# A ring of three fixed score tiles, a new pipeline order, and SyncE places of their own for X copies and the experts' first fetches

## The chip, the cores and the metric

The kernel runs on one core of a Trainium2 chip. The metric is the device time of one execution in microseconds (us). Of the kernel before there are three timed runs and one profiled execution; of the profiled one there is a trace of every engine and DMA queue. The engines are called PE (TensorE), PEld (its weight loads), DVE (VectorE), ACT (ScalarE), POOL (GpSimd) and SP (SyncE, which issues most DMAs).

## What is computed

Attention over 8 batches of 8 heads, 576 tokens and 64 dimensions a head, with rotary embedding of q and k; its output is the input of a mixture of 8 experts of which each token takes one.

```
q_rot, k_rot = rotate(q), rotate(k)
scores = q_rot @ k_rot.T / sqrt(64)
attn = exp(scores - max); attn /= attn.sum + 1e-9
x = (attn @ v)  as 4608 rows of 512
logits = x @ w_gate + modality_bias[modality_id]
e_idx, gate_w = argmax(logits), softmax(logits)[e_idx]
out[mask_e] = gate_w * (relu(x[mask_e] @ w1[e]) @ w2[e])   for each expert e
```

Everything is float32. w1[e] is 512x1024, w2[e] is 1024x512.

## The kernel before, in words

**Work and tiles.** The attention goes over 32 pairs of heads, n = 0 to 31, four pairs to a batch. For one pair SP loads q and k, already laid out with their half-rotated copies, into one of two buffers `R` (`LD`, L121, trace name `ST`), and v (`LV`, L129 and L130). From the third pair on POOL applies the rotary embedding in three passes of 128x1216 (`T1` L212, `T2` L214, `R` L216). The result is split for float32r products: ACT writes the high part (`HI`), POOL the low part (`LO`, L220), both into `HL`. SP copies each part with its two head halves swapped into `SW` (`SWH`, `SWL`, L228, two DMAs each). A buffer `R` is loaded anew for pair n once `LO` of pair n-2 has read it, so `LD` waits on SP for that.

**Scores.** A pair has nine score tiles u = 0 to 8 (`S0` to `S8`, L242), each of two PSUM banks and three products (high-high, low-high, high-low); tile 8 holds the tails of both heads. Behind each come the row minimum on DVE (`MN`, L250; q carries the factor -1/8, so it is the maximum of the scores) and the exponential on ACT (`EX`, L257), which reads the minimum as its bias. Then PE transposes the exponentials by 128x64 blocks into further PSUM tiles of the same ring (`F0` to `F3`, `FA`, `FB`, L263). Bank 0 of such a tile is copied out by ACT (`A_F..`), bank 1 by DVE (`B_F..`, L294), into `PH` and `PD`. The product with v goes in two halves (`AVA`, `AVB`, L318), is copied to `oT` by ACT (`OTA`, `OTB`), turned back and multiplied with the gate's weights by PE (`OUTA`, `OUTB`, L349 and L352), and scaled by DVE into the batch's tile of X (`EVA`, `EVB`, L363 to L369) with the reciprocals of the sums (`RE` on ACT L333, `RI` on DVE). `RE` runs once a pair, which makes it a mark of the period.

The tiles of scores and of transposes come from one pool of three (`psS`, L108): the pool hands them out in turn, and the first write into a tile waits for everything that used it before.

**A batch's end.** After the fourth pair of a batch, X goes to memory with five DMAs on SP (`xout`, one at L374, four at L378). The routing of the batch is a chain of 13 small steps, `rk` 0 to 12, from one engine to the next (L389 to L443): POOL at step 2 (L402 to L405) and step 5 (L416 to L418), ACT at step 3 (`ex`, L409) and step 6 (`ee`, L422), DVE between, PE at step 8, and `oi` on POOL at the end. Five scatters on POOL (L451) then write token and gate into the expert's table `TAB`.

**The experts.** Tokens go through the experts in blocks of 256. The first eight blocks are full blocks of the first six batches; they are planned while the last pairs run (28 small steps `plan`, after pair 23). For a block, SP reads the plan's registers (`m_plan`), fetches the block's rows of the table (`ix`, L583, and `xi`, four DMAs at L586), and, when the expert changes, its w1 and w2 (`m_load1`, `m_load2`). POOL computes indices (`iy`, L592) and gathers the rows of X (L594), eight indirect DMAs per block; DVE transposes them (L635), ACT and DVE split them, and PE computes w1 (L653) and w2 (L670). The first block's fetches, splits and w1 products are placed among the last pairs of the attention.

**The order.** Every job of a pair has a key; job J of pair n is at `key + PER*n`, all jobs are sorted by that, and the order of each engine's queue follows it word by word. On PE, ACT, DVE and POOL this holds for the whole kernel, on SP up to the end of the last pair's own jobs (`dmas.close()`). The routing's keys start at `r0`, a little behind `max(EVA, EVB)` of the batch's fourth pair. `xout` has the key `r0 - 0.01` (L748). Jobs of the experts are placed by `Z(key, ...)`, relative to pair 31. In that block all seven later plans and three table fetches have one key, `ix_` (L775 to L778). The dependencies themselves are found and turned into semaphore waits automatically, whatever the order. The keys are times of a model only in so far as they give the order: an engine does what is next in its queue as soon as its waits are met.

With PER = 14.117 and its keys, the order on SP within a period is `LD`, `SWL`, `LV`, `xout` (each fourth), `SWH`; on POOL `T2`, `R`, `T1`, `LO`; on PE, starting at `S0`: `S0 S5 AVA FA F0 F1 S7 S6 S8 OUTB OUTA F2 F3 FB S4 S2 S1 AVB S3`, where the last five belong to the next pair's scores and this pair's product.

Of the kernel before, what the change touches and what calls it, by code (L numbers as in the profile page):

```python
# [8 lines left out]
F32 = mybir.dt.float32  # L9
# [4 lines left out]
ALU = mybir.AluOpType  # L14
# [4 lines left out]
P = 128  # L19
# [10 lines left out]
K0, Q0, T0, K1 = 0, 288, 800, 928  # L30


PER = 14.117
KEYS = {
# [5 lines left out]
    "FB": 8.50, "A_FB": 9.18, "B_FB": 9.40, "AVA": 14.99, "OTA": 19.19, "AVB": 10.83, "OTB": 16.59, "OUTA": 21.06,  # L40
    "EVA": 24.37, "OUTB": 20.30, "EVB": 21.39, "RE": 11.08, "RI": 16.32, "T1": -34.98, "T2": -27.91, "R": -24.56,
    "LO": -16.92, "HI": -18.39, "SWH": -16.92, "SWL": -12.25, "LD": -41.49, "LV": -10.91,
}
AT = dict(
    rk=(0, 0.6, 1.5, 4.7, 5.5, 6.3, 6.9, 7.5, 9.6, 10.4, 11.2, 14.4, 15.2),
    pl=1.5,
    sc=(10.5, 9.0),
    ix=8.0,
    rows=3.0,
    rows1=-9.0,  # L50
    gap=(3.0, 1.3),
    tr=3.5,
    te=-8.0,
    hi=(-14.0, -9.0, -5.0, -1.0),
# [9 lines left out]
def tile_attention_moe(ctx: ExitStack, tc: tile.TileContext, qk, v, mod, wg, mb, w1, w2, rope, cf, ci, out):  # L64
# [40 lines left out]
    W1 = [wp.tile([P, 4, F], F32R, name=f"W1{c}") for c in "HL"]  # L105
    att = ExitStack()
    pp = att.enter_context(tc.tile_pool(name="pp", bufs=1))
    psS = att.enter_context(tc.tile_pool(name="psS", bufs=3, space=PSUM))  # L108
    psA = att.enter_context(tc.tile_pool(name="psA", bufs=2, space=PSUM))

    st = {}
# [4 lines left out]
    Vs = [pp.tile([P, 2, 5, 64], F32, name=f"V{i}") for i in range(2)]  # L116

    RW = pp.tile([P, 4, 2, 72], F32, name="RW")

    def load(n):  # L120
        nc.sync.dma_start(out=Rs[n % 2], in_=qk[n])  # L121
# [109 lines left out]

    def scores(n, u):
        d = st[n]
        ps = psS.tile([P, 2, 512], F32, name="ps", tag="ps")
        heads = (0, 1) if u == 8 else (u % 2,)
        q0 = T0 if u == 8 else Q0 + u // 2 * P
        L = [(hh, wq, wk) for hh in heads for wq, wk in ((0, 0), (1, 0), (0, 1))]
        for m, (hh, wq, wk) in enumerate(L):
            for g in range(2):
                t = d["HL" if g == hh else "SW"][g * 64:g * 64 + 64]  # L240
                k0 = K1 if g else K0
                nc.tensor.matmul(ps[:, g, 0:288], t[:, wq, q0:q0 + P], t[:, wk, k0:k0 + 288], start=(m == 0), stop=(m == len(L) - 1))  # L242
        if "sum" not in d:
            d["sum"] = sm.tile([P, 9], F32, name="sum", tag="sum")
        d["S", u] = ps

    def rowmin(n, u):
        d = st[n]
        mn = sm.tile([P, 1], F32, name="mn", tag="mn", bufs=6)
        nc.vector.tensor_reduce(mn, d["S", u][:, :, 0:288], op=ALU.min, axis=AX.XY)  # L250
        d["m", u] = mn

    def expo(n, u):
# [6 lines left out]

    def tpose(ps, g, c, src, k0):
        r = slice(g * 64, g * 64 + 64)
        nc.tensor.transpose(ps[:, g, c:c + 64], src[r, k0:k0 + P], idf[r, r])  # L263

    def fill(n, f):
        d = st[n]
        ps = d[f] = psS.tile([P, 2, 512], F32, name="ps", tag="ps")
        if f[1] in "0123":
            j = int(f[1])
            for i in range(8):  # L270
                for g in range(2):
                    tpose(ps, g, i * 64, PJ[j], (S + 64) * (i // 4) + i % 4 * P)
        elif f == "FA":
            for j in range(2):
                for g in range(2):
                    tpose(ps, g, j * 64, PJ[j], 512)
        else:
            for kt in range(4):
                for g in range(2):
                    tpose(ps, g, kt * 64, P4, 64 + g * 64 + kt * P)  # L280
            for g in range(2):
                tpose(ps, g, 256, P4, (1 - g) * S)
            for j in (2, 3):
                for g in range(2):
                    tpose(ps, g, 192 + j * 64, PJ[j], 512)
# [275 lines left out]
    def bank(kind):  # L561
        if kind in banks:
            return banks[kind].tile([P, 512], F32, name=f"ps{kind}", tag=f"ps{kind}")
        if not spare:
            ps = psS.tile([P, 2, 512], F32, name="ps", tag="ps")
            spare.extend(ps[:, i, :] for i in (1, 0))
        return spare.pop()

# [11 lines left out]
    def m_ix(s):  # L580
        d = ms[s]
        ix = d["ix"] = ixp.tile([P, 2, 2], I32, name="ix", tag="ix")
        nc.sync.dma_start(out=ix, in_=TAB[bass.ds(d["r"], BLK), :].rearrange("(p t) w -> p t w", t=2))  # L583
        xi = d["xi"] = ixp.tile([P, 8, 2], I32, name="xi", tag="xi")
        for i in range(4):
            nc.sync.dma_start(out=xi[i * 32:i * 32 + 32], in_=TAB[bass.ds(d["r"], BLK), :].rearrange("(q g) w -> q g w", g=8))  # L586
# [93 lines left out]
    def J(k_, nm, n, f, *a):  # L680
        jobs.append((k_ + PER * n, len(jobs), f, a))
# [32 lines left out]
    for n in range(NPAIR):  # L714
        def K_(nm, f, *a):
            J(K[nm], nm, n, f, *a)

        for u in range(9):
            K_(f"S{u}", scores, n, u)
            K_(f"MN{u}", rowmin, n, u)  # L720
            K_(f"EX{u}", expo, n, u)
        for f in ("F0", "F1", "F2", "F3", "FA", "FB"):
            K_(f, fill, n, f)
            for g in range(2):
                K_(f"{'AB'[g]}_{f}", evac, n, f, g)
        for w in range(2):
            c = "AB"[w]
            K_(f"AV{c}", AV, n, w)
            K_(f"OT{c}", avout, n, w)
            K_(f"OUT{c}", outp, n, w)  # L730
            K_(f"EV{c}", ev, n, w)
        for w in range(2):
            K_("R" + "EI"[w], rsum, n, w)
        if n > 1:
            for part, nm in enumerate(("T1", "T2", "R", "HI", "LO")):
                K_(nm, rope_, n, part)
            for i in range(2):
                K_("SW" + "HL"[i], swap, n, i)
            K_("LV", loadv, n)
        if n > 3:  # L740
            K_("LD", load, n)
        if n % 4 == 1:
            J(r0 - PER, "bias", n, bias, n // 4)
        if n % 4 == 3:
            g = route(n // 4)
            early = n == NPAIR - 9
            r1 = r0 + AT["rk"][-1] + 0.02
            J(r0 - 0.01, "xout", n, xout, n // 4)  # L748
            steps = [(next, g, None)] * NRK
# [12 lines left out]
            for j, (f, *a) in enumerate(scats):
                J(r1 + AT["sc"][early] * j, "sc", n, f, *a)


    def Z(k_, f, *a):
        J(k_, "moe", z, f, *a)

    A = AT
    w1_ = max(r1 + AT["pl"] * 28 - 8 * PER, K["T1"] + 0.1, K["LO"] + 0.1 - PER)  # L770
    ix_ = max(w1_, r1 + A["sc"][1] * 4 + A["ix"] - 8 * PER)
    rows_ = ix_ + A["rows"]
    ga_ = {s * 8 + i: rows_ + A["gap"][0] * i if s == 0 else A["rows1"] + A["gap"][1] * (s * 8 - 8 + i) for s in range(3) for i in range(8)}
    tr_ = [ga_[4 * t + 3] + A["tr"] for t in range(2)]
    te_ = [max(t + 0.6, A["te"]) for t in tr_]  # L775
    Z(w1_, each, m_plan, (0,))
    Z(w1_, each, m_load1, *((0, g) for g in range(4)))
    Z(ix_, m_ix, 0)  # L778
    Z(ix_, each, m_plan, *((s,) for s in range(1, NA)))
    Z(ix_, each, m_ix, *((s,) for s in range(1, 4)))  # L780
    for i in range(8):
        for s in range(3):
            Z(max(ga_[8 * s + i], te_[1] + 0.01) if s == 2 else ga_[8 * s + i], m_gather, s, i // 4, i % 4)
    Z(max(K["LO"] + 0.1, w1_ + 10), each, m_load2, *((0, g) for g in range(4)))
    for g in range(4):
        Z(max(A["hi"][g], w1_ + 10), m_hi, 0, g)
        Z(max(A["hi"][g], w1_ + 10) + 1.3, m_lo, 0, g)
# [1 line left out]
        Z(tr_[t], m_tr, 0, t)  # L789
        Z(te_[t], m_tre, 0, t)  # L790
    for g in range(4):
        l1 = max(A["l1"][g], A["hi"][g] + 1.5, w1_ + 11.5, te_[1] + 1.5)
        Z(l1, m_l1, 0, g)
        Z(l1 + A["l1e"], m_l1e, 0, g)
        Z(end + A["sp2"][g], m_split, 1, g)
# [180 lines left out]
```

## Time and profile before

| | |
|---|---|
| median of 3 runs | 1020.57 us |
| lowest, highest | 1018.56, 1023.85 us |
| profiled execution | 1011.64 us, its span 1009.9 us |
| granted TensorE clock, mean | 0.963 |
| busy: PE, PEld | 924.1 us (92%), 749.4 us (74%) |
| busy: DVE, ACT, POOL | 679.9, 634.1, 666.8 us |

The span runs from the first to the last instruction on the chip. A busy PE includes matmuls at half clock, so its 92% is not all useful work; a stage has to be read with its granted clock beside it. The attention takes the first 564 us or so, with the experts' first blocks from about 482 us on; the rest is the experts.

### The profile page before, as it was taken

How to read it: one execution, taken by the hardware profiler on the slowest of the kernel's cores; microseconds unless marked ns; L12 is line 12 of the kernel's file. 1: busy time of each engine (PE TensorE's matmuls, PEld its weight loads, DVE VectorE, ACT ScalarE, POOL GpSimd, SP SyncE). 2: the span in 40 equal slices, each digit the busy share in tenths (PEclk: the TensorE clock that was granted, in tenths of full speed). 3: DMA queues.
4: the chain of work that ended last, by engine and by line, in shares of the span. 5: the costliest groups of instructions: out<-in, count | busy, mean ns of one | idle time of the engine just before them, and what ended most of it. 6: DMA issues, size and time to landing. Idle time of an engine off the chain costs nothing. (4 is left out here: it accounts for less than half of the span.)

```text
span 1009.9 us, 24801 instructions
## 1 busy us (share of the span) xinstructions
PE 924.1 (92%) x9248; PEld 749.4 (74%) x9248; DVE 679.9 (67%) x1158; ACT 634.1 (63%) x1299; POOL 666.8 (66%) x498
## 2 busy tenths in 40 slices
PE   1999999999999999989558999999999999999996
PEld 1767677676776767757335779888899998888995
DVE  6678678576776777767438277866667766666671
ACT  2778678686877778767437265556566555565661
POOL 7776777887787878889467036666566666655500
PEclk9999899898999999999868899999999999999998
DMA  9666757567575766856554043112261431611100
GB/s 280 188 174 169 194 129 222 133 174 208 139 214 142 191 197 163 216 135 174 161 138 89 2 147 131 43 54 60 66 199 34 135 115 49 215 53 42 45 23 15
DMA packets 73102, 132.70 MB, mean 131 GB/s; under 512 B 29535, under 2 KB 49407, under 8 KB 67984
## 3 DMA queue, kind: packets, MB, share of 16 engines
q1 hardware_dynamic: 62576, 110.33, 39.4%
q0 software_dynamic: 9536, 19.48, 6.5%
q8 instruction: 75, 1.23, 0.6%
q10 hardware_dynamic: 864, 1.25, 0.4%
q14 instruction: 51, 0.42, 0.2%
HBM read 140.59 MB, written 19.77 MB: 159 GB/s over the span
## 5 line engine op out<-in xcount | busy, mean ns | idle before, releaser
L257 ACT ACTIVATE P<-ps,mn 128x576 f32<-128x576 f32 x288 | 210.9, 739 | 126.6 <-DVE mn L250 126.6
L250 DVE TENSOR_REDUCE mn<-ps 128x1 f32<-128x576 f32 x288 | 203.3, 750 | 90.5 <-PE ps L242 90.4
L242 PE MATMUL ps<-SW 64*128 64x288 f32 x960 | 183.3, 326 | 38.3 <-DMA SW<-HL 27.2
L594 POOL DMA_INDIRECT XG<-X,iy x152 | 179.7, 1182 | 49.8 <-issue 39.8
L653 PE MATMUL psH<-HL,W1H 128*128 128x256 f32 x1152 | 202.6, 279 | 0.0
L242 PE MATMUL ps<-HL 64*128 64x288 f32 x960 | 186.7, 323 | 15.4 <-ACT HL L203 15.2
L242 PEld LDWEIGHTS ps<-SW 64*128 64x128 f32 x960 | 139.9, 196 | 61.5 <-DMA SW<-HL 29.8
L653 PEld LDWEIGHTS psH<-HL,W1H 128*128 128x128 f32 x1152 | 176.7, 188 | 1.6
L242 PEld LDWEIGHTS ps<-HL 64*128 64x128 f32 x960 | 143.3, 196 | 27.9 <-ACT HL L203 15.2
L653 PE MATMUL psH<-HL,W1L 128*128 128x256 f32 x576 | 160.8, 279 | 0.7 <-DVE W1L L200 0.7
L318 PE MATMUL pa<-PH,V 128*64 128x256 f32 (+1 forms) x1024 | 150.3, 439 | 0.0
L200 DVE TENSOR_TENSOR W1L<-ST,W1H 128x1024 fp32r<-128x1024 f32 x76 | 90.1, 1222 | 83.3 <-ACT W1H L203 83.3
L674 POOL DMA_INDIRECT out_dram<-y,ix x38 | 40.8, 1074 | 155.1 <-ACT y L673 132.0
L670 PE MATMUL psY<-W2H,SW 128*128 128x512 f32 x304 | 120.3, 396 | 1.3 <-ACT W2H L203 1.3
L670 PE MATMUL psY<-W2L,SW 128*128 128x512 f32 x304 | 120.3, 396 | 0.5 <-DVE W2L L200 0.5
L318 PEld LDWEIGHTS pa<-PH,V 128*64 128x64 f32 x1024 | 71.9, 145 | 55.6 <-issue 22.2
L294 DVE COPY PH<-ps 128x512 f32<-128x512 f32 (+1 forms) x160 | 94.0, 632 | 26.2 <-PE ps L263 25.6
L263 PEld LDWEIGHTS ps<-idf,P 64*128 64x128 f32 x2624 | 89.9, 142 | 26.7 <-ACT P L257 14.5
L653 PEld LDWEIGHTS psH<-HL,W1L 128*128 128x128 f32 x576 | 108.3, 188 | 0.9 <-DVE W1L L200 0.9
L220 POOL TENSOR_TENSOR HL<-ST,HL 128x1216 fp32r<-128x1216 f32 x30 | 83.0, 2768 | 37.7 <-ACT HL L203 34.5
L263 PE MATMUL ps<-idf,P 64*128 64x64 f32 x2624 | 99.6, 229 | 7.1 <-ACT P L257 6.7
L203 ACT ACTIVATE PH<-ps 128x512 f32<-128x512 f32 (+1 forms) x160 | 79.8, 555 | 33.3 <-PE ps L263 32.1
(159 smaller groups left out, 1619.4 us busy)
## 6 DMA issues: line engine op xcount, KB each, us to landing
ST<-in_moe_w_dram SPq DMA_DIRECT2D x152, 512.0 KB
ST<-in_qk_dram SPq DMA_DIRECT2D x31, 1216.0 KB
SW<-HL SPq DMA_DIRECT2D x124, 232.0 KB
V<-in_v_dram SPq DMA_DIRECT2D x64, 128.0 KB
X<-X SPq DMA_DIRECT2D x8, 1024.0 KB
XG<-X,iy POOLq DMA_INDIRECT x152, 2.9
xi<-TAB SPq DMA_DIRECT2D x76, 2.0 KB
V<-in_v_dram SPq DMA_DIRECT2D x64, 16.0 KB
```

The costliest lines, as they stand in the source:

```text
L200: nc.vector.tensor_tensor(o, a, b, op=ALU.subtract)
L203: return nc.scalar.activation(o, i, AF.Copy, scale=scale)
L220: e.tensor_tensor(d["HL"][:, 1, c], a, d["HL"][:, 0, c].bitcast(F32), op=ALU.subtract)
L242: nc.tensor.matmul(ps[:, g, 0:288], t[:, wq, q0:q0 + P], t[:, wk, k0:k0 + 288], start=(m == 0), stop=(m == len(L) - 1))
L250: nc.vector.tensor_reduce(mn, d["S", u][:, :, 0:288], op=ALU.min, axis=AX.XY)
L257: nc.scalar.activation(p.rearrange("p (a b) -> p a b", a=2), ps[:, :, 0:288], AF.Exp, bias=d.pop(("m", u)), scale=-1.0, accum_out=d["sum"] ...
L263: nc.tensor.transpose(ps[:, g, c:c + 64], src[r, k0:k0 + P], idf[r, r])
L294: mine.append((nc.vector.tensor_copy if g else acopy)(o, i).ins)
L318: nc.tensor.matmul(pa[hh * 64:hh * 64 + 64, 0:c1 - c0], d["V"][:, hh, kt, :], r, start=(kt == 0), stop=(kt == 4))
L594: nc.gpsimd.indirect_dma_start(out=XG[s % 2][:, t, g, :], out_offset=None, in_=X.rearrange("n (i f) -> (n i) f", f=P)[0:rows], in_offset=b ...
L653: nc.tensor.matmul(ps[:, i, :], w[:, c, f0:f0 + P], x[:, c, :], start=(m == 0), stop=(m == 11))
L670: nc.tensor.matmul(ps, hx[:, c, t * P:(t + 1) * P], w[:, c, :], start=(m == 0), stop=(m == 23))
```

## The change

- The three score tiles are fixed now, one PSUM pool with `bufs=1` and three names. `ring()` hands them out in turn. A tile's last row minimum is remembered, and PE's writes into the tile are declared free of it: they wait for the exponential, which itself waited for the minimum. Waits of a refill are by the regions written, no longer by the whole pool tile.
- PER and all keys of the pair's jobs are new. The order on PE within a period is now `S0 AVB S2 S5 S4 OUTB OUTA F3 F0 FA F2 FB F1 S8 S1 S6 AVA S7 S3` (from `S8` on the next pair's scores and this pair's `AVA`; `AVB` is the previous pair's); on POOL `T2`, `R`, `T1`, `LO`; on SP `SWL`, `LD`, `LV`, `SWH`, `XO` (each fourth).
- `xout` has a key of its own, `XO`.
- `xi` is fetched with one DMA whose source is repeated four times, in place of four DMAs.
- Plans, table fetches and loads of the experts' first blocks have a key each. The first block's w1 products come behind the last scores and transposes.

```diff
-PER = 14.117
+PER = 14.438
 KEYS = {
...
+    "S0": 0.00, "MN0": 1.75, "EX0": 3.14, "S1": -4.26, "MN1": -2.77, "EX1": -1.95, "S2": 3.22, "MN2": 3.92, "EX2":
+    4.72, "S3": -0.39, "MN3": 0.21, "EX3": 2.42, "S4": 4.17, "MN4": 5.26, "EX4": 6.18, "S5": 3.77, "MN5": 4.59,
+    "EX5": 5.46, "S6": -3.75, "MN6": -2.10, "EX6": -1.23, "S7": -0.95, "MN7": 0.88, "EX7": 1.70, "S8": -5.22, "MN8":
+    -4.02, "EX8": -2.91, "F0": 6.57, "A_F0": 7.38, "B_F0": 7.37, "F1": 8.69, "A_F1": 9.59, "B_F1": 9.85, "F2": 7.62,
+    "A_F2": 8.41, "B_F2": 8.41, "F3": 5.81, "A_F3": 6.90, "B_F3": 6.78, "FA": 7.17, "A_FA": 7.86, "B_FA": 7.96,
+    "FB": 8.21, "A_FB": 8.89, "B_FB": 9.00, "AVA": 11.22, "OTA": 13.98, "AVB": 14.84, "OTB": 18.19, "OUTA": 19.77,
+    "EVA": 25.51, "OUTB": 19.01, "EVB": 20.38, "RE": 11.27, "RI": 15.89, "XO": 27.00, "T1": -32.78, "T2": -26.38,
+    "R": -23.03, "LO": -15.27, "HI": -18.83, "SWH": -17.41, "SWL": -11.79, "LD": -39.33, "LV": -10.14,
 }
 AT = dict(
...
-    ix=8.0,
-    rows=3.0,
-    rows1=-9.0,
-    gap=(3.0, 1.3),
...
+    w1=(1.0, 5.7, 8.0, 10.2),
+    w2=(-8.0, -5.0, -2.0, 1.0),
+    plan=(-99.0, -15.0, 4.0, 6.0, 8.0, 10.0, 12.0, 14.0),
+    ix=(-16.5, -9.5, 4.0, 6.0),
+    rows=4.0,
+    gap=1.3,
 )
...
-    psS = att.enter_context(tc.tile_pool(name="psS", bufs=3, space=PSUM))
+    psS = att.enter_context(tc.tile_pool(name="psS", bufs=1, space=PSUM))
...
+    RING = [psS.tile([P, 2, 512], F32, name=f"ps{i}") for i in range(3)]
+    lastmin = [None] * 3
+    turn = [0]
+
+    def ring():
+        i = turn[0] % 3
+        turn[0] += 1
+        seen, lastmin[i] = lastmin[i], None
+        return i, RING[i], seen
+
+    def free(inst, seen):
+
+        if seen is not None:
+            tc.declare_no_dep(inst.ins, seen, reason="the exponential waited for the minimum")
...
-                nc.tensor.matmul(ps[:, g, 0:288], t[:, wq, q0:q0 + P], t[:, wk, k0:k0 + 288], start=(m == 0), stop=(m == len(L) - 1))
+                free(nc.tensor.matmul(ps[:, g, 0:288], t[:, wq, q0:q0 + P], t[:, wk, k0:k0 + 288],
+                                      start=(m == 0), stop=(m == len(L) - 1)), seen)
...
-        nc.tensor.transpose(ps[:, g, c:c + 64], src[r, k0:k0 + P], idf[r, r])
+        free(nc.tensor.transpose(ps[0][:, g, c:c + 64], src[r, k0:k0 + P], idf[r, r]), ps[1])
...
-        for i in range(4):
-            nc.sync.dma_start(out=xi[i * 32:i * 32 + 32], in_=TAB[bass.ds(d["r"], BLK), :].rearrange("(q g) w -> q g w", g=8))
+        nc.sync.dma_start(out=xi, in_=TAB[bass.ds(d["r"], BLK), :].rearrange("(q g) w -> q (g w)", g=8).unsqueeze(0).to_broadcast([4, 32, 16]))
...
-            J(r0 - 0.01, "xout", n, xout, n // 4)
+            K_("XO", xout, n // 4)
...
-    ix_ = max(w1_, r1 + A["sc"][1] * 4 + A["ix"] - 8 * PER)
...
+    ix_ = [max(w1_, r1 + A["sc"][1] * 4 + 8 - 8 * PER, t) for t in A["ix"]]
+    ga_ = {s * 8 + i: ix_[s] + A["rows"] + A["gap"] * i for s in range(3) for i in range(8)}
...
-    Z(w1_, each, m_load1, *((0, g) for g in range(4)))
-    Z(ix_, m_ix, 0)
-    Z(ix_, each, m_plan, *((s,) for s in range(1, NA)))
-    Z(ix_, each, m_ix, *((s,) for s in range(1, 4)))
+    for g in range(4):
+        Z(w1_ + A["w1"][g], m_load1, 0, g)
+        Z(max(K["LO"] + 0.1, w1_ + 10, A["w2"][g]), m_load2, 0, g)
+    for s in range(NA):
+        if s:
+            Z(max(ix_[0], A["plan"][s]), m_plan, s)
+        if s < 4:
+            Z(max(ix_[s], A["plan"][s] + 0.01), m_ix, s)
...
-    Z(max(K["LO"] + 0.1, w1_ + 10), each, m_load2, *((0, g) for g in range(4)))
...
-        l1 = max(A["l1"][g], A["hi"][g] + 1.5, w1_ + 11.5, te_[1] + 1.5)
+        l1 = max(A["l1"][g], A["hi"][g] + 1.5, w1_ + 11.5, te_[1] + 1.5, max(K[f] for f in K if f[0] in "SF") + 0.1 * g + 0.1)
```

More of the change, by code (lines that the diff above doesn't have):

```diff
@@ L30 @@
 K0, Q0, T0, K1 = 0, 288, 800, 928
-PER = 14.117
+PER = 14.438
 KEYS = {
[5 rows of a table removed]
-    "FB": 8.50, "A_FB": 9.18, "B_FB": 9.40, "AVA": 14.99, "OTA": 19.19, "AVB": 10.83, "OTB": 16.59, "OUTA": 21.06,
-    "EVA": 24.37, "OUTB": 20.30, "EVB": 21.39, "RE": 11.08, "RI": 16.32, "T1": -34.98, "T2": -27.91, "R": -24.56,
-    "LO": -16.92, "HI": -18.39, "SWH": -16.92, "SWL": -12.25, "LD": -41.49, "LV": -10.91,
[5 rows of a table added]
+    "FB": 8.21, "A_FB": 8.89, "B_FB": 9.00, "AVA": 11.22, "OTA": 13.98, "AVB": 14.84, "OTB": 18.19, "OUTA": 19.77,
+    "EVA": 25.51, "OUTB": 19.01, "EVB": 20.38, "RE": 11.27, "RI": 15.89, "XO": 27.00, "T1": -32.78, "T2": -26.38,
+    "R": -23.03, "LO": -15.27, "HI": -18.83, "SWH": -17.41, "SWL": -11.79, "LD": -39.33, "LV": -10.14,
 }
@@ L233, in scores @@
         d = st[n]
-        ps = psS.tile([P, 2, 512], F32, name="ps", tag="ps")
+        ri, ps, seen = ring()
+        d["ring", u] = ri
         heads = (0, 1) if u == 8 else (u % 2,)
@@ L249, in rowmin @@
         mn = sm.tile([P, 1], F32, name="mn", tag="mn", bufs=6)
-        nc.vector.tensor_reduce(mn, d["S", u][:, :, 0:288], op=ALU.min, axis=AX.XY)
+        lastmin[d["ring", u]] = nc.vector.tensor_reduce(mn, d["S", u][:, :, 0:288], op=ALU.min, axis=AX.XY).ins
         d["m", u] = mn
@@ L262, in tpose @@
         r = slice(g * 64, g * 64 + 64)
-        nc.tensor.transpose(ps[:, g, c:c + 64], src[r, k0:k0 + P], idf[r, r])
+        free(nc.tensor.transpose(ps[0][:, g, c:c + 64], src[r, k0:k0 + P], idf[r, r]), ps[1])
     def fill(n, f):
         d = st[n]
-        ps = d[f] = psS.tile([P, 2, 512], F32, name="ps", tag="ps")
+        ps = ring()[1:]
+        d[f] = ps[0]
         if f[1] in "0123":
@@ L564, in bank @@
         if not spare:
-            ps = psS.tile([P, 2, 512], F32, name="ps", tag="ps")
+            ps = ring()[1]
             spare.extend(ps[:, i, :] for i in (1, 0))
@@ L770, in tile_attention_moe @@
     w1_ = max(r1 + AT["pl"] * 28 - 8 * PER, K["T1"] + 0.1, K["LO"] + 0.1 - PER)
-    ix_ = max(w1_, r1 + A["sc"][1] * 4 + A["ix"] - 8 * PER)
-    rows_ = ix_ + A["rows"]
-    ga_ = {s * 8 + i: rows_ + A["gap"][0] * i if s == 0 else A["rows1"] + A["gap"][1] * (s * 8 - 8 + i) for s in range(3) for i in range(8)}
+    ix_ = [max(w1_, r1 + A["sc"][1] * 4 + 8 - 8 * PER, t) for t in A["ix"]]
+    ga_ = {s * 8 + i: ix_[s] + A["rows"] + A["gap"] * i for s in range(3) for i in range(8)}
     tr_ = [ga_[4 * t + 3] + A["tr"] for t in range(2)]
```

5 rows, old and new, of the table KEYS are left out of this document.

## The prediction, made before the change was run

> **What bounds the kernel now.** I read the page's engine shares first, then the windows of each stage, then the chain, the waits of PE and the timelines of SP and POOL around one stall.
>
> ```profile
> span 1009.9 us, 24801 instructions
> 82.58:97.92 15.34, 15.01 (x210) 11.04 (x209) 11.57 (x24) 12.10 (x33) 11.37 (x5) 1.00 0.62 164
> 97.92:112.91 14.99, 13.51 (x193) 9.83 (x191) 12.13 (x31) 11.94 (x33) 10.08 (x11) 1.00 0.85 244
> 112.91:132.46 19.55, 18.49 (x215) 13.24 (x217) 11.40 (x25) 11.64 (x32) 15.90 (x9) 0.83 0.51 132
> 132.46:147.33 14.87, 14.54 (x206) 10.73 (x206) 11.09 (x24) 11.64 (x31) 12.05 (x5) 1.00 0.64 169
> 132.46:481.94 349.48, 330.96 (x4475) 242.63 (x4475) 254.66 (x551) 260.39 (x684) 286.27 (x182) 0.97 0.67 176
> 481.94:563.77 81.83, 54.44 (x627) 39.92 (x623) 42.70 (x83) 39.78 (x97) 46.53 (x45) 0.79 0.45 117
> 563.77:584.10 20.33, 18.18 (x133) 14.83 (x133) 4.47 (x13) 4.10 (x9) 0.00 (x0) 0.83 0.00 1
> 584.10:1004.00 419.90, 415.39 (x2646) 372.97 (x2646) 284.26 (x326) 244.39 (x297) 233.35 (x195) 1.00 0.27 86
> ```
>
> A row of the windows gives its bounds and length, the busy time (and instructions) of PE, PEld, DVE, ACT and POOL, the granted clock, the DMA share and the rate. The bounds of the attention rows are the starts of successive `re` activations, of which each head pair has one, so a row is one period of the pipeline. There are four facts. The MoE part, 419.90 us, keeps PE at 415.39 with full clock: nothing of the change reaches it. A plain attention period (14.87) is PE-bound too, with 14.54 busy. One period in four, the one after a batch's routing, takes 19.55 at clock 0.83; the four together take 64.75. The 22 periods from 132.46 on take 349.48, 15.89 each, 63.5 per four. Last, the three periods in which the experts' first blocks are fetched, 481.94 to 563.77, take 81.83 with PE busy for 54.44; the tail behind them 20.33 at clock 0.83.
>
> What makes the 19.55, in windows of the stall and the queues just before it:
>
> ```profile
> 111.50:113.50 2.00, 0.06 (x1) 0.00 (x0) 1.40 (x7) 1.71 (x5) 0.92 (x1) 0.93 0.58 141
> 113.50:120.00 6.50, 6.36 (x31) 3.89 (x33) 2.20 (x3) 2.28 (x6) 6.18 (x6) 0.50 0.44 97
> ```
> ```profile
> 85.56 0.34 SPq L121 DMA_DIRECT2D ST<-in_qk_dram  x1
> 85.95 1.10 SPq L228 DMA_DIRECT2D SW<-HL  x2
> ...
> 97.27 0.34 SPq L374 DMA_DIRECT2D X<-X  x1
> 97.66 4.43 SPq L378 DMA_DIRECT2D X<-XT  x4
> 102.20 1.19 SPq L228 DMA_DIRECT2D SW<-HL  x2
> 103.48 0.53 SPq L121 DMA_DIRECT2D ST<-in_qk_dram  x1
> 104.06 1.44 SPq L228 DMA_DIRECT2D SW<-HL  x2
> ```
> ```profile
> PE ps L242 <- DMA SW<-HL: 27.2, 10, 10.8
> PE ps L242 <- DVE PD L294: 6.7, 20, 0.4
> ```
>
> The X copies of the batch (L374, L378) hold SP from 97.27 to 102.1; the swaps of HL (L228) wait behind them, and PE stands still for 2.00 us at 111.50 for `SW`. Behind the idle the clock is 0.50 for 6.50 us: half of PE's pace for that long loses 3.25 at most, and I take 2.7, since the window's 19.55 less 14.87 is 4.7 and 2.0 of it is idle. The waits say the same: 27.2 us over 10 waits of PE for `SW<-HL`. No row has PE waiting for `mn`.
>
> **The change, part by part.** *Ring and minimum.* A score tile is now refilled without waiting for the minimum, and each bank of an evacuated tile by itself. Nothing in the waits ends on `mn`, so the first is 0. The second can take some of PE's 6.7 us on `PD`, 20 waits: at most 6.7/32 = 0.2 per period; taken as 0.1.
>
> *The new order of a period.* The same instructions in another order; PE's 14.54 stays the floor. But a second loop gets tight. In the new keys the swap of `LO` (SWL) goes to SP right ahead of the next load (LD), which needs the `LO` before the last; LD must land, then T1 and LO run on POOL, then SWL again; before, LD went first. Rows for its terms:
>
> ```profile
> 92.63 2.78 POOL L212 TENSOR_TENSOR ST<-ST,ST 128x1216 f32<-128x1216 f32 x1 [1.50 <-DMA ST<-in_qk_dram]
> 97.62 2.78 POOL L220 TENSOR_TENSOR HL<-ST,HL 128x1216 fp32r<-128x1216 f32 x1 [2.21 <-ACT HL L203]
> 100.35 0.26 POOL L402 TENSOR_TENSOR dl<-lg,mx 128x40 f32<-128x40 f32 x1
> ...
> 112.58 2.75 POOL L212 TENSOR_TENSOR ST<-ST 128x1216 f32<-128x1216 f32 x1 [3.57 <-DMA ST<-in_qk_dram]
> ```
>
> From issue of LD to T1: 85.56 to 92.63, 7.07, in a plain period; 103.48 to 112.58, 9.10, where swaps and X copies share the DMA engines (share 0.85 there). The loop is SWL's issue 1.10 + (7.07 to 9.10) + T1 2.78 + LO 2.78 = 13.7 to 15.8. In the new order a swap always goes just ahead of LD, so I take 7.75, a third of the way up: 14.4. It lies about level with PE's 14.54. A plain period comes to 14.55 (14.87 less 0.1 for the banks, less 0.2 because the slack of PE in that row, 14.87 - 14.54 = 0.33, is a wait that the new order places elsewhere): 4 x 14.55 = 58.2.
>
> *X copies.* They have a key behind SWH now, so the 4.9 us of SP stand behind the swap that PE wanted at 111.50. That stall (4.7) goes. What is late next is the routing. Its steps are alternating small operations of ACT, DVE and POOL, placed by keys that start at EVA, and EVA moved. In the old order `ee` (step 6 on ACT, L422) stands behind OTB; in the new one (17.99 against 18.19) it stands ahead of it. It needs step 5 on POOL, which is queued behind T2:
>
> ```profile
> 101.35 2.79 POOL L214 TENSOR_TENSOR ST<-ST 128x1216 f32<-128x1216 f32 x1
> 104.10 0.26 POOL L416 TENSOR_TENSOR vv<-vv,vm 128x40 f32<-128x40 f32 x1
> ...
> 104.69 0.23 POOL L418 TENSOR_SCALAR OH<-vv 64x8 bf16<-64x8 f32 x1
> ```
> ```profile
> L203 ACT ACTIVATE oT<-pa 128x320 f32<-128x320 f32 x64 | 26.0, 406 | 4.2 <-PE pa L318 4.2
> ```
>
> T2 has the key 16.94 there, so step 5 on POOL begins at 16.94 + 2.79 = 19.7 and ends 0.8 later (from 104.10 to 104.69 + 0.23). ACT stands from 17.99 to about 20.5 with OTB behind it; OUTB on PE (19.01) needs OTB. That leaves PE idle for 1.9 (20.5 + 0.41 for OTB - 19.01) to 4.0, and by the rows at 111.50 and 113.50 half clock behind it for 2.7; 4.0 is twice the wait at 111.50, for a queue of PE that runs dry earlier. I take 2.5 + 2.7 = 5.2. Further, scatter 4 and the POOL operations of step 2 stand between T1 and LO now, where before (100.35) they followed LO; I add 0.5 for that once in four periods, two operations of 0.26. Four periods: 58.2 + 5.2 + 0.5 = 63.9 against 63.5 before: no gain in the attention ahead of the transition. The bounds are 58.7 with nothing in the stall's place (58.2 + 0.5), and 65.4 with 4.0 idle.
>
> *The experts' first fetches.* Rows of the block that goes:
>
> ```profile
> 493.67 2.01 SPq L586 DMA_DIRECT2D xi<-TAB  x4
> ...
> 507.81 0.36 SPq L583 DMA_DIRECT2D ix<-TAB  x1
> ...
> 515.65 0.50 SPq L228 DMA_DIRECT2D SW<-HL  x1
> 500.11 0.27 POOL L592 TENSOR_SCALAR iy<-xi,CF 128x8 int32<-128x8 int32 x1 [11.88 <-DMA xi<-TAB]
> ```
>
> Between 493.67 and 515.65 SP holds first blocks' tables, seven plans (to 507.81) and three more tables, and the last swap of the pairs waits behind all: 22 us. POOL stands 11.88 of them for `xi`, with rope behind it. The change spreads the plans by key, two ahead of the last swap and six from key 4 on, where no swap is left; `xi` is one issue in place of four (2.01 to about 0.5). So the 22 us stall and POOL's 11.88 go. What comes: the low halves of W1 on DVE, and the transposes of the gathered rows, which wait for the gathers:
>
> ```profile
> L200 DVE TENSOR_TENSOR W1L<-ST,W1H 128x1024 fp32r<-128x1024 f32 x76 | 90.1, 1222 | 83.3 <-ACT W1H L203 83.3
> L594 POOL DMA_INDIRECT XG<-X,iy x152 | 179.7, 1182 | 49.8 <-issue 39.8 <-POOL iy L592 5.5 <-DVE HL L200 3.0
> ```
> ```profile
> XG<-X,iy POOLq DMA_INDIRECT x152, 2.9
> ```
>
> Four splits of 1.22 on DVE, half hidden: 2.5. The gathers (1.18 each, 2.9 more to land) now have a closer place to the transposes on DVE, and a DVE that waits holds minima and evacuations behind it: 4.5 idle, then 2.7 half clock, 7.2. Sum: 3 x 14.55 = 43.65 + 5.2 (the routing of the batch before it) + 2.5 + 7.2 = 58.5 against 81.83: 23 saved. Bounds: 46 if neither wait appears (36 saved), 70 if the gathers block twice and a swap is late again (12 saved). The tail, 20.33 at clock 0.83, keeps full clock if no idle precedes it: 20.33 x 0.17 = 3.4, taken as 3.
>
> *Sum.* With 63.9 against 63.5 counted as 0: 0 - 23 - 3 = -26. The profiled execution took 1011.64 (span 1009.9) and comes to 985.6; the median of the runs, 1020.57, is 8.9 above it, so the forecast is 994.
>
> [...]
>
> **The rivals.** *Nothing replaces the stall.* ACT has enough in hand at `ee` that OUTB is never late; the rest as above. For it: ACT is busy for only 11.64 of a plain period. Against it: the keys put `ee` 1.7 us ahead of what it waits for. Four periods 58.7 against the mean 63.5, over 28 periods -33.6; transition -33 (23, the 5.2, and 4.7 of the gathers' 7.2); tail -3: 1020.57 - 69.6 = 951.
>
> [...]
>
> *The saving is given back in the transition.* DVE waits for gathers, POOL for tables, and the first blocks come as late as now: for it, 152 gathers already have 49.8 us idle before them. Then 1012 to 1020: no difference.
>
> *Slower: the buffer loop binds.* If LD takes 9.10 from issue to T1 in every period, since a swap goes ahead of it each time, the loop is 15.76 and PE (14.54) no longer the bound. It decides from an LD of about 8.9 on (loop 15.6, where the mean period with a stall removed gains nothing more). Four periods cost 4 x 15.76 + 5.2 + 0.5 = 68.7, 5.2 more than 63.5, 36 over 28 periods; with the 26 saved and no tail gain the time is about 1030.
>
> **How the numbers follow.** Forecast 0.55, nothing replaces the stall 0.17, whole clock 0.05, given back 0.11, slower 0.12. 0.5% is 5.1 us, about what a measurement of this kernel can tell from no change (the three runs span 1018.56 to 1023.85). The forecast's own bounds, 12 to 36 saved in the transition and four periods 1.5 dearer or 2.5 cheaper than taken, about half the way to 58.7 (7 x 1.5 = 10 up, 7 x 2.5 = 17 down), give 964 to 1015. The range goes from 955, which takes in the upper half of the first rival, to 1022, which takes in the given-back case; left out are half of 0.17 and the slower 0.12. Faster: 0.55 + 0.17 + 0.05 and 0.03 of the given-back case, 0.80; same 0.08; slower 0.12.
>
> **What would show it.** On SP, the X copies behind the swaps of HL and no wait of PE for `SW` behind them; `re` periods of 14.5 in three of four; in the fourth, 19 to 20, ACT waiting at L422 for POOL with PE idle ahead of OUTB and clock 0.50 after it. In the transition no block of plans ahead of the last swap, and DVE waiting at the transposes for `XG`. Periods of 15.7 with POOL waiting for `ST<-in_qk_dram` at T1 would show the slower rival; four periods below 60 the first. The forecast is wrong if the routing period has no idle, or if the transition keeps over 75 us.

## The result, and the profile after

The changed kernel takes 982.36 us (median of 4 runs, 978.22 to 993.34) against 1022.21 us (1018.56 to 1024.86) for the kernel before on the same chip: a ratio of 0.960, 95% interval 0.955 to 0.965, so some 40 us less. The ratio leaves out the slow run of 993.34, which is over 1.5% above the fastest of its kernel. In a later group of runs (y3 below) the changed kernel took 993.92 (988.55 to 1002.45) against 1021.37: 0.975, interval 0.970 to 0.980, 27 us less. The forecast was 994, in a range of 955 to 1022.

The profiled execution took 978.22 us against 1011.64. Here are its span and the windows that answer to those of before, bounded in the same way by the starts of `re` (columns: length, busy PE, PEld, DVE, ACT, POOL, granted clock, DMA share, rate).

```profile
span 976.4 us, 24969 instructions
97.61:112.76 15.15, 14.29 (x206) 10.65 (x204) 11.80 (x30) 11.91 (x33) 10.06 (x11) 1.00 0.80 244
112.76:127.30 14.54, 14.38 (x206) 10.75 (x204) 10.94 (x25) 11.49 (x32) 13.42 (x8) 1.00 0.54 171
127.30:464.90 337.60, 321.83 (x4482) 241.48 (x4481) 251.70 (x553) 259.14 (x683) 288.45 (x182) 0.99 0.63 182
464.90:524.71 59.81, 47.70 (x593) 33.98 (x591) 41.05 (x84) 39.36 (x96) 34.57 (x35) 0.91 0.53 151
524.71:550.96 26.25, 21.00 (x154) 15.91 (x153) 5.10 (x15) 4.72 (x10) 10.31 (x11) 0.87 0.12 21
550.96:971.00 420.04, 415.42 (x2646) 372.96 (x2646) 284.21 (x326) 244.03 (x297) 233.21 (x195) 1.00 0.26 86
```

The transition into the experts begins at 464.90 where it began at 481.94: the attention ahead of it gained 17.0. The transition's three periods take 59.81 in place of 81.83: 22.0. The tail takes 26.25 in place of 20.33: 5.9 lost. The experts take 420.04 in place of 419.90. Together 33.0 less, of a difference of 33.5 between the spans. (The profiled run of before was 9 to 11 us below that kernel's medians, the one of after 4 below its own, hence 33 here and 40 in the medians.)

The period that took 19.55 at clock 0.83 is gone. The period that held the routing, 97.61 to 112.76, takes 15.15, the one behind it 14.54, both at full clock. The queue of SP there, start and length of each group of issues:

```profile
97.25 2.09 SPq L246 DMA_DIRECT2D SW<-HL  x2
99.44 0.54 SPq L395 DMA_DIRECT2D X<-X  x1
100.03 4.48 SPq L399 DMA_DIRECT2D X<-XT  x4
104.60 1.20 SPq L246 DMA_DIRECT2D SW<-HL  x2
105.85 0.58 SPq L139 DMA_DIRECT2D ST<-in_qk_dram  x1
```

The X copies are behind the swap of HI, as forecast. But one thing more has changed place, of which the prediction counted only the cost: the second pair of swaps (of LO) goes ahead of the load, where before it went behind it (103.48 and 104.06). How much that matters is in the packets of the trace. A swap's packets have 3712 bytes, the load's 9728. Before, the swap issued at 104.06 had its first packet at 109.12 and its last at 113.09, 9.0 us after its issue, behind the load's packets that began at 105.21; PE's first product behind the wait started at 113.64. Now the swap issued at 104.60 has its packets from 105.82 to 107.94, done 3.3 us after its issue, and the load's begin at 107.63.

Two more views of the changed kernel belong to the forecast's steps. First ACT around `ee` (L443), which was to wait for POOL, and POOL (the second fence) in the same routing:

```profile
103.72 0.20 ACT L277 ACTIVATION_READ_ACCUMULATOR P<-ps,mn 128x1 f32 x1
103.82 0.74 ACT L277 ACTIVATE P<-ps,mn 128x576 f32<-128x576 f32 x1
104.44 0.21 ACT L277 ACTIVATION_READ_ACCUMULATOR P<-ps,mn 128x1 f32 x1
104.53 0.30 ACT L443 ACTIVATE ee<-es,EPS 128x5 f32<-128x5 f32 x1
104.72 0.44 ACT L221 ACTIVATE oT<-pa 128x320 f32<-128x320 f32 x1
```
```profile
99.42 0.26 POOL L423 TENSOR_TENSOR dl<-lg,mx 128x40 f32<-128x40 f32 x1 [2.78 <-DVE mx L420]
...
105.90 0.26 POOL L437 TENSOR_TENSOR vv<-vv,vm 128x40 f32<-128x40 f32 x1
```

`ee` starts at 104.53 without any idle ahead of it, 1.4 us before POOL even begins step 5 at 105.90. Then DVE, and PE, in the transition:

```profile
510.96 0.71 DVE L655 STREAM_TRANSPOSE XG<-XG 128x512 f32<-128x512 f32 x1 [3.41 <-DMA XG<-X,iy]
```
```profile
516.07 0.40 PE L261 MATMUL ps<-HL 64*128 64x288 f32 x1 [4.03 <-ACT P L277]
```

DVE waits 3.41 for the gathered rows with minima queued behind it, ACT then waits for the minima, and PE stands for 4.03; the clock is 0.50 for 3.4 us behind that. This is the second of two such waits. The first came a period earlier, at the first half of the gathers:

```profile
501.00 0.71 DVE L655 STREAM_TRANSPOSE XG<-XG 128x512 f32<-128x512 f32 x1 [1.76 <-DMA XG<-X,iy]
```
```profile
499.39 0.37 PE L261 MATMUL ps<-SW 64*128 64x288 f32 x1 [1.25 <-issue]
502.44 0.58 PE L261 MATMUL ps<-HL 64*128 64x288 f32 x1 [2.38 <-DVE XG L655]
```

PE stands for 1.25 and 2.38 there, and the clock is 0.50 for 6.83 us from 500.1 on. ("issue" marks idle time in which the engine waited for nothing that the profile shows.)

### The profile page after: what moved, and what is told of

It is laid out like the page before. It is cut to its first block, busy times and chain, and to the rows that moved or that the text cites. A ratio compares the mean times of both kernels' runs of the same rounds, so it can differ in the third digit from the quotient of the medians.

```text
span 976.4 us, 24969 instructions
## 1 busy us (share of the span) xinstructions
PE 908.2 (93%) x9248; PEld 742.4 (76%) x9248; DVE 674.2 (69%) x1158; ACT 632.3 (65%) x1299; POOL 663.8 (68%) x498
## 3 DMA queue, kind: packets, MB, share of 16 engines
q10 hardware_dynamic: 864, 1.25, 0.4%
## 5 line engine op out<-in xcount | busy, mean ns | idle before, releaser
L261 PE MATMUL ps<-HL 64*128 64x288 f32 x960 | 170.7, 315 | 29.8 <-ACT HL L221 14.9
L261 PE MATMUL ps<-SW 64*128 64x288 f32 x960 | 170.3, 316 | 9.0 <-DMA SW<-HL 4.7
L261 PEld LDWEIGHTS ps<-HL 64*128 64x128 f32 x960 | 137.7, 190 | 53.2 <-ACT P L277 15.9
L261 PEld LDWEIGHTS ps<-SW 64*128 64x128 f32 x960 | 135.4, 190 | 24.4 <-ACT P L277 14.1
L339 PE MATMUL pa<-PH,V 128*64 128x320 f32 (+1 forms) x1024 | 142.2, 420 | 1.1 <-PE ps L261 0.7
L694 POOL DMA_INDIRECT out_dram<-y,ix x38 | 39.1, 1030 | 143.6 <-ACT y L693 129.8
L283 PE MATMUL ps<-idf,P 64*128 64x64 f32 x2624 | 105.3, 229 | 8.8 <-DVE PH L315 2.4
L283 PEld LDWEIGHTS ps<-idf,P 64*128 64x128 f32 x2624 | 92.6, 141 | 22.7 <-ACT PH L221 8.6
L315 DVE COPY PH<-ps 128x512 f32<-128x512 f32 (+1 forms) x160 | 97.3, 632 | 17.4 <-PE ps L283 10.9
L221 ACT ACTIVATE PH<-ps 128x512 f32<-128x512 f32 (+1 forms) x160 | 84.0, 556 | 22.1 <-PE ps L283 14.9
L218 DVE TENSOR_TENSOR W2L<-ST,W2H 128x1024 fp32r<-128x1024 f32 x76 | 92.4, 1220 | 4.1 <-ACT W2H L221 3.6
```

The source lines that it names most:

```text
L218: nc.vector.tensor_tensor(o, a, b, op=ALU.subtract)
L221: return nc.scalar.activation(o, i, AF.Copy, scale=scale)
L261: free(nc.tensor.matmul(ps[:, g, 0:288], t[:, wq, q0:q0 + P], t[:, wk, k0:k0 + 288], start=(m == 0), stop=(m == len(L) - 1)), seen)
L283: free(nc.tensor.transpose(ps[0][:, g, c:c + 64], src[r, k0:k0 + P], idf[r, r]), ps[1])
L315: mine.append((nc.vector.tensor_copy if g else acopy)(o, i).ins)
L339: nc.tensor.matmul(pa[hh * 64:hh * 64 + 64, 0:c1 - c0], d["V"][:, hh, kt, :], r, start=(kt == 0), stop=(kt == 4))
```

## The experiments

Each kernel ran beside the kernel before on one chip; the first four share a chip, the next four another, the last four a third. The kernel before took 1020.41, 1002.15 and 1021.37 us on these, so times are compared within a group, and stages by the traces. The changed kernel itself ran with the result and in the last group, not on the chips of x1 to x8. Each run has one trace. Two stretches serve throughout: the 20 attention periods from the third `re` to the 23rd, and the stretch from the 29th `re` to the first product with w2, transition and tail together. These are their rows for the two kernels, the first two of before, the next two of after. A difference of a few us between two single traces is only a hint: the five kernels with the old order of the pair and the load ahead of the swap (before, x1 to x4) take 312.96 to 320.55 in the 20 periods, and the four with the old order and the old fetches (before, x1, x3, y1) 102.14 to 117.93 in the other stretch.

```profile
67.69:386.34 318.65, 303.27 (x4074) 222.22 (x4074) 230.77 (x501) 236.59 (x621) 252.99 (x147) 0.96 0.66 177
481.94:584.08 102.14, 72.60 (x759) 54.73 (x756) 47.15 (x96) 43.86 (x105) 46.53 (x45) 0.80 0.36 94
```
```profile
67.57:370.67 303.10, 291.16 (x4078) 218.43 (x4077) 226.42 (x502) 235.47 (x622) 251.81 (x147) 1.00 0.63 186
464.90:550.96 86.06, 68.69 (x745) 49.89 (x742) 46.15 (x97) 44.08 (x105) 44.88 (x46) 0.90 0.41 112
```

### The parts alone, in the old order

**X copies alone (x1).**

```diff
-    ... "LD": -41.49, "LV": -10.91,
+    ... "LD": -41.49, "LV": -10.91, "XO": 25.50,
-            J(r0 - 0.01, "xout", n, xout, n // 4)
+            K_("XO", xout, n // 4)
```

> The kernel before with one thing changed: the X copies have a key just behind the swap of HI. Theory: the attention's gain (17 us up to the start of the transition) is the removed wait of PE for the swapped tile and its half clock, whatever the order of the pair: 17 to 23 us faster than before, and the waits of PE for SW<-HL fall from 27.2 us to about 11. Rival: the new order of the pair carries it, since in the old order the load behind the X copies is late instead: at most 8 us faster.

It took 1028.98 us; ratio 1.011 (1.003 to 1.018): not faster, but about 1% slower. The 20 periods and the waits of PE in them:

```profile
65.49:383.42 317.93, 297.61 (x4076) 218.82 (x4073) 230.85 (x501) 237.21 (x621) 253.82 (x147) 0.98 0.66 177
```
```profile
PE ps L242 <- DMA SW<-HL: 13.3, 5, 5.1
```

PE waits for the swap as before: 13.3 us over 5 waits, the longest 5.1. The queue of SP ahead of that longest one:

```profile
217.99 1.12 SPq L228 DMA_DIRECT2D SW<-HL  x2
219.20 2.99 SPq L374 DMA_DIRECT2D X<-X  x1
222.24 3.44 SPq L378 DMA_DIRECT2D X<-XT  x4
225.78 0.55 SPq L121 DMA_DIRECT2D ST<-in_qk_dram  x1
226.37 1.14 SPq L228 DMA_DIRECT2D SW<-HL  x2
```

The swap of HI goes first now. But the X copies end where the load and the swap of LO stand; that swap, issued at 226.37 behind the load, has its first packet at 231.46, and PE's wait ends at 237.10. The theory that the gain is the swap of HI freed from the X copies has fallen: they leave the other swap late, behind the load.

**The fetch keys alone (x2)**, with the table fetch left at four DMAs: the blocks `w1`, `w2`, `plan`, `ix`, `rows`, `gap` and the `Z(...)` lines of the change, on the old keys of the pair.

> The kernel before with the spread keys of the experts' first fetches alone (table fetch still four DMAs, old order, old X copies). Theory: the transition's 22 us come from this alone, the tail gives some 4 back: 15 to 20 us faster. Rival: the keys only fit the new order, and PE still waits for the swap behind the X copies of that batch: at most 8 us faster.

It took 1001.68; ratio 0.984 (0.976 to 0.991), 19 us less. Transition and tail take 93.50, where the kernels x1 and x3, with old fetches in the old order, take 114.36 and 117.9 and the profiled run of before 102.14. So the fetches are worth 9 to 24 us of the trace without the new order.

**The ring alone (x3)**: `psS` with `bufs=1`, `ring()`, `free()`, nothing else. By its code, the first block's w1 products lie in a ring tile that a later transpose writes over before they are read, so that part of the output comes out different; the change keeps them apart by placing them behind the last transposes.

> The kernel before with the ring of three fixed tiles alone. Theory: no wait ended on the minimum, so only PE's 6.7 us on the evacuation PD can go: 0 to 5 us faster. Rival: the ring carries the attention's gain: 12 us faster or more.

It took 1023.52; ratio 1.006 (1.002 to 1.009): not faster. The waits for `PD` are gone from the list, but 11.1 us over 7 waits for `SW<-HL` are in it, where before had 9.8 over 5.

**All but the order of the pair (x4)**: the changed kernel with the old PER and keys, X copies as in x1.

> The changed kernel with PER and the keys of the pair as before (X copies at the key of the first run): everything but the new order. Theory: the order is worth nothing by itself and the parts add up: 980 to 988 us. Rival: the order is needed: 995 us or more.

It took 1009.63; ratio 0.988 (0.981 to 0.996). The 20 periods take 320.55, no less than before. Ring, X copies and fetches together bring 11 us of the change's 27 to 40, no more than the fetches alone in x2; the parts do not add up, and the rest needs the new keys.

### The new order, with one part undone

**Without the ring (x5)**: tiles from a pool of three again.

> The changed kernel with its score tiles from the pool of three, as before the change; all keys stay. The ring was worth nothing in the old order. Theory: it is worth little here too, since no wait of PE ended on the minimum: 0 to 5 us slower than the changed kernel's 982 (982 to 987). Rival: the new order was made for the ring and stands without it: 994 or more, with new waits of PE for an evacuation or an exponential in every period.

**X copies at their old key (x6)**, `J(r0 - 0.01, "xout", ...)`.

> The changed kernel with the X copies at their old key, ahead of the swap of HI. Theory: the new order gains in the attention because SP has room for the X copies (4.9 us) between the swap of HI and its next job, 5.6 us by the keys where the old order had 3.7; ahead of the swap PE stands still for it again: seven stalls of 2 to 4.7 us, 997 to 1015. Rival: the new order of PE asks for the swapped tile so late that the place doesn't matter: at most 990.

**The old block of fetches (x7).**

> The changed kernel with the old keys of the experts' first fetches (all seven plans and three tables in one block). Theory: the transition's 22 us hang on the block, since PE waited there for a swap behind it: 998 to 1008. Rival: the order makes up for it: at most 988.

The times on this chip are 973.95 (972.32 to 978.28) without the ring, 977.74 (974.28 to 980.64) with the X copies first, and 991.79 (988.35 to 993.70) with the old fetches. The rows, in this order, one kernel a fence:

```profile
68.20:369.87 301.67, 292.07 (x4075) 218.39 (x4072) 225.26 (x501) 234.64 (x622) 250.92 (x146) 0.99 0.64 186
464.73:544.86 80.13, 66.62 (x744) 49.75 (x741) 45.78 (x96) 44.04 (x105) 46.06 (x46) 0.91 0.48 120
```
```profile
69.20:374.77 305.57, 292.58 (x4074) 220.79 (x4073) 226.03 (x501) 235.79 (x621) 252.01 (x147) 0.99 0.64 185
468.58:546.94 78.36, 64.77 (x744) 48.50 (x742) 46.04 (x97) 43.96 (x105) 44.02 (x46) 0.93 0.46 123
```
```profile
69.56:375.53 305.97, 293.53 (x4074) 221.72 (x4073) 226.72 (x501) 235.65 (x621) 251.24 (x147) 0.98 0.63 184
469.83:563.82 93.99, 66.92 (x744) 50.73 (x742) 46.23 (x97) 43.79 (x105) 47.55 (x46) 0.84 0.41 102
```

In the 20 periods none of the three parts matters: 301.67, 305.57 and 305.97 beside 303.10 and 307.58 of the changed kernel in its own two groups. Neither the ring nor the place of the X copies carries the attention's gain, and the theory of x6 has fallen. The old fetches cost 14 to 16 us in transition and tail against the other two (93.99 against 80.13 and 78.36), as the theory of x7 said in kind: 14 to 18 in the times. What they do is in the waits of PE:

```profile
493.55 0.20 PE L448 MATMUL pa<-OH,UT 128*128 128x48 bf16 x1 [13.55 <-POOL OH L437]
...
504.16 0.61 PE L259 MATMUL ps<-SW 64*128 64x288 f32 x1 [5.88 <-DMA SW<-HL]
```

The step of the routing on PE waits 13.55 for POOL, which itself waits 12.4 for `xi` ahead of it, and a swap behind the block of plans costs another 5.88.

**The third block's gathers later (x8):** `ix=(-16.5, -9.5, 24.0, 24.0)` in place of `(-16.5, -9.5, 4.0, 6.0)`.

> The changed kernel with the table fetch and the gathers of the third block (slot 2) moved from key 4 to key 24, out of the stretch from 525 to 538 us in which PE has six waits for issue (3.8 us) with half clock behind them. Theory: the gathers' packets delay what PE is fed with, and both go: 3 to 8 us faster than the changed kernel, 974 to 979, and no wait for issue on PE there. Rival: the waits for issue belong to that place in PE's own instructions, whatever POOL does: they stay, and the time is 980 to 985.

It took 984.65 (982.18 to 988.31), 7 to 11 us more than x6 and x5 beside it, and the 974 to 979 of its theory were missed. PE has no waits for issue in the tail here, but x5 and x6 have none there either, with the gathers where the change put them: so the gathers are not shown to be the cause. The time was lost in the experts' part, 430.56 us against 420.06 in x6. PE waits there once 5.09 us for a weight (`W1H`), and behind it, from 575.71 to 582.08, pairs of its products start mostly 0.64 us apart, where it was 0.35 ahead of the wait: SP took 13.75 us, from 564.90 on, for the four loads of a w1 that took it 4.88, from 559.94 on, in x6.

### Which way round the swap and the load go

The prediction had noted the order of LO's swap and the load and priced it as a delay of the load. After x1 to x8 all kernels without waits for the swap had the swap ahead of the load; but all of them had the rest of the new order too. So this one place was changed alone, in both kernels.

**The old kernel, load behind the swap (y1):** `"LD": -40.285` in place of `-41.49`.

> The kernel before with one key changed: LD goes to SP behind the swap of LO instead of ahead of it; the order of PE, ACT, DVE and POOL is the old one. Theory: what made PE wait at 111.50 was less the 4.9 us of the X copies than the 1.2 MB of the load: the swap issued at 104.06 behind it had its packets from 109.12 to 113.09. Ahead of the load it lands some 3 us after its issue, the waits for SW<-HL up to the transition go, and periods 2 to 28 take 397 to 405 us in place of 414: 10 to 17 us faster. Rival: the new order of PE carries the gain, and the load, now later, makes POOL late instead: 411 or more, within 5 us of the kernel before.

**The changed kernel, load ahead of the swap (y2):** `"LD": -40.79` in place of `-39.33`.

> The changed kernel with one key changed: LD goes to SP ahead of the swap of LO, as before the change. Theory: the waits of PE for SW<-HL come back in each batch, with half clock behind the longer ones: periods 2 to 28 take 408 to 416 us in place of 397, 11 to 19 us slower than the changed kernel. Rival: the new order of PE has room for the late swap: at most 402 and within 5 us of the changed kernel.

**The changed kernel again (y3).**

> The changed kernel itself, as a measure for the others of this call and for the size of the change on this chip. On the chip of the runs x5 to x8 the kernel before took 1002 us where it took 1020 to 1022 on others. Theory: the kernel before varies because the same stalls of about 2 us do or don't halve the clock; the changed kernel, with few stalls of that length, stays at 970 to 985. Rival: the chips differ in everything by the same per cent: the ratio to the kernel before stays at 0.96 wherever it runs.

The times are 1016.95 (1015.65 to 1024.25), 1015.39 (1009.19 to 1019.21) and 993.92 (988.55 to 1002.45); the kernel before 1021.37. Rows and waits of the 20 periods, y1, y2, then y3's row:

```profile
68.11:377.66 309.55, 295.38 (x4074) 217.99 (x4074) 230.69 (x501) 236.77 (x621) 250.86 (x146) 0.99 0.63 182
```
```profile
67.68:390.54 322.86, 300.99 (x4071) 224.56 (x4070) 226.28 (x501) 236.34 (x622) 253.87 (x147) 0.96 0.68 175
```
```profile
PE ps L261 <- DMA SW<-HL: 12.9, 8, 3.1
```
```profile
68.33:375.91 307.58, 292.94 (x4078) 219.63 (x4076) 227.08 (x502) 236.24 (x621) 251.79 (x147) 0.99 0.63 183
```

One key moved takes 21 of the changed kernel's 27 us away: y2 is slower than y3 by 21.5 (1015.39 - 993.92), with PE waiting for `SW<-HL` again (8 waits, 12.9 us) and the clock at 0.96. In one routing of y2 the load is issued at 103.73 and the swap at 104.32; the swap's packets come at 109.20 to 112.22, behind the load's from 104.90 on. In y1 the waits for `SW<-HL` are gone from these periods too, though the X copies still go ahead of the swap of HI; they take 309.55, and 6.5 us of waits for `P` have come. Its whole time does not move (ratio 0.998, 0.994 to 1.002; the theory had 10 to 17 us): the 9 us by which these periods are below those of before, 318.65, stand against 112.35 for transition and tail, 10 above before's trace and in line with 114.36 and 117.93 of x1 and x3, which have the old fetches too. Whether the swap's place alone is worth anything in the old order these runs do not settle.

The packets say the same in three traces: the swap (0.2 MB a piece), issued 0.6 us behind the load's 1.2 MB, has its first packet 5.1 us after its issue in before (104.06 to 109.12) and in x1 (226.37 to 231.46), 4.9 us in y2 (104.32 to 109.20). Ahead of the load, in the changed kernel, it has it 1.2 us after (104.60 to 105.82). By what mechanism the load delays the swap, the traces do not show.

Across all fourteen traces (before, after and the twelve): in the 20 periods PE has waits for `SW<-HL`, 9.8 to 14.2 us of them, in each of the six with the load ahead of the swap, and none in the eight with the swap ahead. The six take 313 to 323 us, with the old order or the new; old order with the swap ahead 309.6; the new with the swap ahead 301.7 to 307.6. So in these periods the new order without the swap's place is worth nothing (322.86). The swap's place is worth 15 in the new order (y2 against y3); in the old one it is 3 to 11 by the traces, which the time of y1 does not confirm. Both together come to 5 to 19.

As to y3's own question, neither theory nor rival holds. The ratio moved from 0.960 to 0.975 while the kernel before stayed at 1021 to 1022, so it is the changed kernel that is 12 us slower here (303.10 against 307.58 in the 20 periods, 86.06 against 89.43 in transition and tail). What makes it so stays open.

**Routing step 2 behind LO (y4):** `rk=(0, 0.6, 2.7, ...)` in place of `1.5`.

> The changed kernel with step 2 of the routing (three small operations of POOL) behind LO instead of ahead of it. In the changed kernel POOL waited there 2.78 us for the maximum of DVE with LO queued behind. Theory: LO, its swap and the next load come some 3 us earlier in one period of four; since PE has little idle there (0.8 us), it gains 0 to 4 us. Rival: the steps behind it come later, and PE waits longer for OH (2.2 us now): 2 to 8 us slower.

It took 997.07 (990.19 to 1002.82), no better than y3. The 20 periods take 304.09; transition and tail 99.06 instead of 89.43. By the times, POOL's wait of 2.78 ahead of LO costs PE nothing that can be seen.

## Why the prediction was right, and where it wasn't

**The sum.** It forecast 26 less; the runs gave 40 and 27. By stages of the profiled runs it was forecast 0, 23 and 3 for attention, transition and tail, and came 17.0, 22.0 and -5.9. So the total came near the forecast partly by luck: a gain that was not foreseen and a loss that was not foreseen offset each other in part, and that y3 hit 994 to the microsecond says nothing for the mechanism.

**The attention, forecast 0, came 17.0.** Two steps failed. The first: "It needs step 5 on POOL, which is queued behind T2", said of `ee`. It needs `es` alone, which DVE makes in step 4; `OH` of step 5 goes to PE in step 8. The trace has `ee` without a wait. The stall of 5.2 per batch, which made the forecast 0, doesn't exist. What came in its place is smaller: 2.2 us of PE for `OH` in all of the 20 periods, and waits of at most 1.0 for evacuations. The second: "The X copies of the batch (L374, L378) hold SP from 97.27 to 102.1; the swaps of HL (L228) wait behind them, and PE stands still". The stall's place was right and its cause incomplete. (Of the 27.2 us of waits quoted for it, 10.8 are one wait of the transition; the 20 periods have 9.8.) It was the swap of LO that PE waited for, with its first packet at 109.12, where the load's had begun at 105.21. The prediction's rows had the issue at 104.06 and the end of the idle at 113.50, 9.4 us, and no step asked what the swap did in that time. The edit's sign was turned by this: the swap ahead of the load was priced at 0.68 us of delay for the load, and was what removed the stall (y2 undoes it).

Most of the gain is clock, not idle time. Of the 15.5 us that the 20 periods are shorter (318.65 to 303.10), 12.1 are in PE's busy time (303.27 to 291.16, for the same products): before, 23.9 us of these periods ran at clock 0.50, after none. PE's idle time fell only from 15.4 to 11.9, since small waits came for the 9.8 us of waits for the swap that went.

The buffer loop came out about as priced: the load issued at 105.85 had T1 at 112.69, 6.84 later, the one at 86.32 7.52 later; over the 20 periods it was 6.5 to 9.5, in the middle 6.8, and taken was 7.75. POOL waited for the load at each T1 there, 40.0 us in 20 waits, which, together with periods of 15.7, the prediction had named as a sign of the slower rival; but PE had no wait for a swap behind it. A plain period was forecast at 14.55. Single periods reach that (14.54), but the 20 take 15.16 on average, 14.56 of PE busy and 0.60 idle, so the wait that "the new order places elsewhere" stayed, in small pieces. Without the stall of 5.2 and with the dearer plain periods, four periods take 60.6 there, against 63.9 in the forecast. The ring and the minimum were rightly put at about nothing (x3, x5).

**The rival that nothing replaces the stall** had the mechanism of the attention right. In size the truth lies halfway: 58.7 per four periods there, 63.9 in the forecast; 337.60 over 22 periods is 61.4. It was a chance of 0.17 in a forecast that had the wrong dependency at 0.55.

**The transition, forecast 23 less, came 22.0 less**, and its main step held: no block ahead of the last swap (x7 shows what the block costs). What came in its place was priced half rightly. DVE's wait for the gathers came as forecast, with 4.03 us idle and 3.4 of half clock, 1.7 lost, where 4.5 and 2.7 lost were taken. But the gathers blocked twice, which the forecast had only in its upper bound: the first time cost PE 1.25 and 2.38 idle and 6.83 of half clock that began within the idle, some 2.2 lost. The 5.2 of the routing's stall, which did not come, made room for this in the sum; the closeness of 22 to 23 owes something to that. Whether the fetches give all this without the new order was not asked: in the old order transition and tail take 93.50 (x2) and 101.68 (x4), against 86.06 and 89.43 (y3).

**The tail, forecast 3 less, came 5.9 more.** The step "The tail, 20.33 at clock 0.83, keeps full clock if no idle precedes it" left out that the first block's w1 products are moved behind the last transposes by an edit of the diff itself: a group of about 3 us that lay ahead of it. The other part is six waits of PE for "issue", 3.8 us, between 534 and 540, and 6.83 us of clock 0.50 from 537.61 on; in y3 there are such waits in the same stretch of the tail (2.8 us in seven, from 540 to 546), in x5 to x8 none. Their cause stays open.

**Short idles and half clock.** In the changed kernel idles of 2.75 and 4.03 us were each followed by 3.41 us of clock 0.50 (from 424.97 and 517.13 on), so the case of a whole clock, 0.05 in the forecast, fell: the new idles of that length did not leave the clock whole. But the forecast's fixed 2.7 lost behind each such idle did not hold: in y2 an idle of 1.43 us (to 112.92) had 3.41 us of half clock behind it, in x6 one of 2.68 us (to 429.21) had none. **The slower rival** fell: the 20 periods take 15.16 on average, not 15.76, without a wait of PE for a swap. (Its sum of 1030 had the tail's 3 in the 26 saved, though it names no gain in the tail; without it the sum is 1034.)

## What to carry to other kernels

The order of two DMAs issued one right behind the other on one queue is a decision. Here the swap's last packet came 9.0 us after its issue behind the load and 3.3 us ahead of it: where a small transfer that an engine will want soon stands behind a large one that has time, try it ahead, and read the wait from issue to last packet, not from the issue slots alone. When a stall has a queue of causes (copies, load, swap), moving the first can hand the wait to the next, as in x1 (9.8 us of waits for the swap before, 13.3 there); undo one at a time in the good kernel to see which one holds. And follow a dependency to the tile that is read, not to the step that precedes it in a list.

## What was not expected of the hardware

In the traces every stretch at clock 0.50 within the attention and the transition is a multiple of 3.41 us: 3.41, 6.83, 10.24 or 13.65, and once each 20.5 in x2, 23.9 in x4, and 27.3 in x7 and y4. In the kernel before, idles of 1.6 to 2.4 us ahead of such stretches gave 6.83 three times, 3.41 twice and none once, so that the same stall cost 1.1 to 4.9 us over a plain period. So one and the same stall differs by almost 4 us within one execution. The kernel before also took 1002 us on one chip and 1020 and 1021 on two others; whether this has to do with it is not shown, since it was traced on one chip only.
